# Weight tiles of 576 columns in place of 1152, and a new list of operations

## The chip, the core and the metric

The kernel runs on one core of a Trainium2 chip. The metric is the device time of one execution in microseconds. The engines are written as in the profile: PE is the matrix engine (TensorE), PEld its weight loads, DVE the vector engine, ACT the scalar engine, POOL the general engine (GpSimd), and SP the engine that issues the transfers.

## What is computed

Two halves of an output of 2048 rows and 1152 columns, all in float32. Columns 0 to 575 are a long convolution (an S4D state-space layer), columns 576 to 1151 a linear attention with a learned softmax feature map. The reference, cut to that:

```python
# left half: A_u is [1, 2048, 576]
P = jnp.exp((A * dt[:, None])[:, :, None] * pos[None, None, :])
K = 2.0 * jnp.einsum("dn,dnl->dl", C, P).real
y = jnp.fft.irfft(jnp.fft.rfft(u_t, L2) * jnp.fft.rfft(K, L2)[None], L2)[:, :, :L]
left = y + u * D_skip
# right half: x is [1, 2048, 576], 32 heads of 18
q, k, v = x @ wqkv                       # split in three
phi_q = softmax of q @ w_phi and of its negative, side by side (36 features)
phi_k = the same of k @ w_phi
kv = jnp.einsum("bhsf,bhsd->bhfd", phi_k, v);  z = phi_k summed over s
right = (phi_q @ kv / (phi_q @ z + 1e-6)) @ wo
```

## The kernel before, in words

The left half is done as a transform of 4096 points in stages of small matrix products. `u_first(k)` (16 of them, named u0 to u15 here) loads a block of the signal into a tile `ub`, multiplies it by `w1` on PE, copies the sums from PSUM to a tile `zi` and stores that in DRAM. `group(g)` (36, worked in 18 pairs, "group 0" to "group 17") makes a piece of the convolution's kernel: POOL adds phases, ACT takes sines and exponentials, DVE multiplies, and PE sums (`g0` are the products with `sel`, `g4` the sums). `k_first`, 16 `product` units and 16 `last` units finish the transform.

The right half is done in tiles of 128 rows. A **key tile** (16) loads a block of x transposed (`load_x`: tile `zo`, then split into a high part and a remainder in `x9`), multiplies it by the key weights and by the value weights (`gemm_halves`: two halves of 288 columns, 14 matrix products each: high weights with high x, low weights with high x, high weights with the low x), takes the double softmax, and adds into the 18x36 sums per head. Then `kv` writes those sums to DRAM and reads them back in another layout (`kvb`). A **query tile** (16) does the same with the query weights, divides, transposes, and multiplies by the output weights.

Weights come as a pair of tiles, high part and low part. `fold` makes the key (and later the query) weights: five blocks of `wkT` are loaded into staging tiles, PE multiplies each by the feature map (`fT`), ACT copies the high part out of PSUM and DVE subtracts to get the low part. `whole` makes the value (and later the output) weights: three thirds of 192 columns are loaded, ACT copies the high part and DVE or POOL subtracts. Before the change one pair `wh`, `wl` of 1152 columns holds keys in columns 0 to 575 and values in columns 576 to 1151. The pools keep one buffer for each of the two names, so the pair for queries and output takes the place of the pair for keys and values.

Nothing is scheduled at run time. Each operation gets a number as it is described, 2,506 in all, and the text `ORDER` lists these numbers in the order in which they are handed to the engines; an engine works its instructions strictly in that order. A number can carry `x` (run on the other engine of two allowed ones), `@` and digits (which of PSUM's eight banks its result takes) and `:n` (n filler products on PE ahead of it, 128x256 in bf16, on a tile of zeros, at L244; they write a bank that the operation then overwrites, or add zeros). The list before has 87 fillers: 20 and 11 of them at the start, between the blocks of the first fold, and 56 later.

Of the kernel before, what the change touches and what calls it, by code (L numbers as in the profile page):

```python
# [25 lines left out]
KEPT = 8  # L26
# [257 lines left out]
def body(tc, nc, i, out, ctx):  # L284
# [10 lines left out]
    tags({1: "zero ident w1 hp quarter dsk kvb fT cst wh wl ks sel pa ax ay mn ldc",  # L295
# [56 lines left out]
    def weights():  # L352

        return B("wh", [128, 5, 2 * D], F32R), B("wl", [128, 5, 2 * D], F32R)
# [27 lines left out]
    def whole(src, w, done, stage, eng):  # L382
        hi, lo = w

        def third(c):
            cs, half = slice(D + 192 * c, D + 192 * c + 192), Mark()
            wi = B(stage[c], [128, 5, 192])
            load_rows(wi, src, slice(192 * c, 192 * c + 192), 192)
            op("act", c_act(960), lambda: act.activation(hi.t[:, :, cs], wi.t, AF.Copy), r=[wi], w=[done[c], half], with_=[hi])
            op(eng, c_pool(960) if eng == "pool" else c_dve(960), lambda: (pool if eng == "pool" else dve).tensor_tensor(  # L390
                lo.t[:, :, cs], wi.t, hi.t[:, :, cs].bitcast(F32), op=ALU.subtract), r=[wi, half], w=[done[c]], with_=[hi, lo], lock=True)
# [39 lines left out]
    def gemm_halves(x, w, done, c0):  # L431
        ps = B("ps", [128, 2, 288], banks=2)
        for c, (cs, need) in enumerate(zip(halves, done)):
            gemm(x, w, need, ps, lambda c=c: ps.t[:, c], slice(c0 + cs.start, c0 + cs.stop))
# [33 lines left out]
    wkv, have_k, have_v = weights(), marks(5), marks(3)  # L468
    pl.at("fold", 0)
    fold(i["wkT"], wkv, have_k, ("e", "e", "cs", "e", "kvb"), [])  # L470
    pl.at("fold", 1)
    whole(i["wv"], wkv, have_v, ("zi", "zi", "cs"), "dve")
# [9 lines left out]
    def key_tile(t):  # L482
# [5 lines left out]
        pk = gemm_halves(x, wkv, (have_k[0:3], have_k[2:5]), 0)  # L488
        pc = gemm_halves(x, wkv, (have_v[0:2], have_v[1:3]), D)
# [47 lines left out]
    wqo, have_q, have_o = weights(), marks(5), marks(3)  # L537
    fold(i["wqT"], wqo, have_q, 5 * ("e",), [opened])
    pl.at("fold", 3)
    whole(i["wo"], wqo, have_o, 3 * ("e",), "pool")  # L540

    def query_tile(t):
        pl.at("query", t)
        ps = gemm_halves(load_again(t) if t < KEPT else load_x(t), wqo, (have_q[0:3], have_q[2:5]), 0)
# [49 lines left out]
        po = gemm_halves(o9, wqo, (have_o[0:2], have_o[1:3]), D)  # L594
# [399 lines left out]
0 1 2 4 3 1185 1125 5x 1124 34 35@0:20 69 1131 1135 1134 1132 36 39 37 44 1136 6 1133 1137 1138 1139 1140 38 1155 1141 40 1156 1147 359 27 8@2 1142  # L994
360 28@4:11 20 1168 51 13 47 1143 1144 1145 361x 1146 29 21@6 22 1106 362x 32 30 1148 1149 1154 1150 1151 1152 7 1105 33 31 15@0 52 25 23 9 24 279 41
26 14 45 18 10 1095 1108 1153 1157 16 17 1166 19 1158 364@4 48 11 1159 12 46 280 281x 49 1160 53 54 57@6 56 1192 42 1109 1167 1110 43 1161 1162 282
1107 1112 1163 60 61 1111 63 1113 62 363 368 299 1024 1164 1165 55 59@0 365@2 366 1035 367 72 1116 1114 1186 64 1118 369 1193 377 1115 300 58 1117
1119 370 371x 1120 1121 73 372 376 301x 1096@64 1194 1195 1098x 70 1187 1188 373 284@2 1196 65 1431 302 1197 1230 66 67 1189 1231 1190 1123 1097 1232
1223 283 1198 1224 1191 1036@40 303@6 288 1038x 177 1233 1037 287 374 68 1169 50@4 1200 304 1126 308 286@0 375x 1199 71 307 289 290 309 285 297x 378
1170 74x 1225 75x 1226 1201 1122 1179 1178 178 1227 1171 1182@52 1183@36 1211 1127 179x 1202 310 1128 1214 114 305@0 306 78@6 1203 1205 1204 1208 1206  # L1000
77 1435 296 180 291 379 1234 1039 76 1235 292 317 293 1228 182@0 311 1229 82 312 183 294 81 1207 313 295x 83 314 1184@52 1209@3 115 187 298 186 188
1213 1212 1215 116 1236 117 1237 181 339 1210x 189 195 1262 315x 184@6 316 119@0 120 1434 1432 1238 1129 1433 1172 1437 1217 1216 318 1218@5 1220@32
1173 1239 1174 1436 190x 185 1240 1438 84 1439 123 124 125 1268 126 1219 1243 1175 196 1241 90 127x 1269 85 1270 340 380 118 1244 191 341 342 79@0
1221@56 1271 1261 1263 1264 1272 1242 128 219 1249 80 1080 122@2 91 1246 1265 1266 343@0 1245 192 121 198 1273 193 1252 1222@57 220 1267 194 197 1275
86 129 87 88 1247@6 133 1248 221 1176 222 130 1251 1255 344 348 132 1274 224@2 223 131x 1254 1440 1250 1253 1276 227 89x 1177 228 199 200 229 1307 347
1277 346@6 134 1441 350 349 345 1259@52 351x 1258@30 319 230 201x 357 1256@1 92 356 231 1299 1306 1287 1290 1280 203@6 1279 93 1278 1281 1283 320 1257
1282 202 204 208 1308 1309 1442 232 352 207 209 1284 226@2 225 237 233 94 1081@06 1082 1083x 1084 1260@52 234 1310 1300 1130 1301 1285@3 210 1302 1303
1311 1304 1305 1312 1314x 95 96 1288 205@0 1286x 1289 235x 1338 1292 353 1293 1181 99@6 236 1313 1315 238 98 354 1180 239 1443 206 1291 1478 1296@53
355x 1316 1455 1317 103 102 104 1294@2 1295 211 321 212 217x 1100 1337 1339 1340 1101@60 358 1319 105 1345 1344 1346 1347 1297@25 1447 1102x 1103
1298@67 1320 100@0 106 1325 1328 1318 1321 1322 1348 1349 213 107 101 214 1323@5 322 323@2 1324x 108 1350 1070 1090 111 1341 240 324 241 112 1326 216  # L1010
1352 1327 1329 109 328 327 1342 97 1330 329 1331 259 1099 325@0 1343 1351 1454 326 215x 1071@26 242 260 1353 1456 110x 1332@5 218 1072 395 1444 1445
1446 1448 1449 1451 1450 135 1073 337 1452 1453 261x 1104 1091@26 1093x 1335@01 1092 1334@23 1457 1458 1459 1460 1354 330 331 244@6 1355 1333 1384
1357 262 136 1356 1358 1359 1360 1523 1461 1462 1463 1464 1465 243 1524 1525 1526 1387 246@2 1492 1094 247 1361@5 248 1362 113 156 1363 249 250 251x
332 245 257 157 1364@06 137x 1366 264@2 1336@56 333 334 158 1365x 263 265@0 1386 1389 1390 1531 336 1530 1385 252 267 268 269 1388 1050 1074 1479 335x
270 338 1369@62 1368 266 1367 1030 159 1493 1370x 277x 1532 1533 138 1527 1528 1529 1534 271 1535 1371 1379@26 1391@5 1381x 1380 1374@02 253 1537 272
273 1485 1536 1372 1373 276 256 1538x 1486 1375 274 1487 275x 1488 1376x 160 1383 141@6 140 1392 144 145 147 162@0 146 1489 1494 1495 1496 1497 1498
161 148 254 1490 1539 1382 1051@26 166 1053 165 278 1520@56 1052x 1540 167 1521@72 1378 440 1542 1541 168 255x 143@0 1500 1543 1544 1545 1546 149 1549
169 142 154 258 1552 1522@53 170 1031@60 1054 150 151 396 1040 1065 1032 1547@2 164@6 1551 1554 163 1033 174 1491 1499x 1548 1555 1377 153 171 172
1550 175x 1066@02 152x 398@6 397 1568 1553 1569 1501 1556@5 1068x 173x 399 1034 401 1067x 402 155 176 1482@23 475 1502 400 1503 417 1041@06 1570 1571
# [77 lines left out]
```

## Time and profile before

| | |
|---|---|
| time, median of 3 runs | 555.22 us (551.48 to 556.59) |
| the profiled execution's own time | 554.43 us |
| its span, first to last instruction | 552.5 us |
| mean granted PE clock | 0.990 |
| busy: PE, DVE, ACT, POOL | 534.8, 457.3, 377.2, 331.7 us |
| DMA, busy share of 16 engines | 64.8% |
| moved | 111.07 MB |

The profile is a record of one execution. Busy times of an engine are unions of its instructions. A matrix product's record is longer than its share of the engine, because products overlap in the array: the distance from one product's start to the next tells what it costs. "PEclk" is the clock that the throttle granted, as a share of the full clock. A row of the timeline has the start, the duration from the first start to the last end, engine, line, operation, tiles and count; in brackets stands the idle time ahead of it and what ended that.

### The profile page before, as it was taken

The page shows a single profiled execution, that of the slowest core. Times are in us where ns is not written, and L with a number is a line of the kernel's source. Part 1 is how long each engine was busy: PE and PEld are TensorE (multiplying, and loading weights), DVE is VectorE, ACT ScalarE, POOL GpSimd, SP SyncE. Part 2 cuts the span into 40 slices and gives each one's busy share as a digit, 9 for nine tenths or more (in the row PEclk, how much of TensorE's full clock was granted, in tenths as well). Part 3 has the DMA queues.
Part 4 walks back from the last instruction along what each step waited for, and adds up shares of the span by engine and source line. Part 5 has one row for each costly group of instructions (what it writes and reads, how often), then busy time and mean ns, then how long its engine had stood idle before and what let it go on. Part 6 is the DMA issues. An engine that isn't in the chain of part 4 may idle for free.

```text
span 552.5 us, 18491 instructions
## 1 busy us (share of the span) xinstructions
PE 534.8 (97%) x7777; PEld 439.9 (80%) x7777; DVE 457.3 (83%) x756; ACT 377.2 (68%) x546; POOL 331.7 (60%) x476
## 2 busy tenths in 40 slices
PE   6999999999999799999999999999999999999997
PEld 4999999989888677888887775777886866676986
DVE  6899999799978698999899988889885678676542
ACT  3789577998549789699699967968973343413332
POOL 2397767886499948782569778686534363444300
PEclk8999999999999998999999999999999999999999
DMA  8951710263464767726664678656788889998786
GB/s 216 296 173 53 259 59 26 94 194 135 147 171 151 234 214 245 216 86 193 210 205 142 212 231 243 200 173 224 210 249 245 232 268 303 283 310 259 264 255 160
DMA packets 90368, 111.07 MB, mean 201 GB/s; under 512 B 5938, under 2 KB 74546, under 8 KB 90286
## 3 DMA queue, kind: packets, MB, share of 16 engines
q1 hardware_dynamic: 90286, 109.90, 64.8%
q8 instruction: 61, 1.00, 0.7%
q14 instruction: 21, 0.17, 0.1%
HBM read 65.34 MB, written 44.54 MB: 199 GB/s over the span
## 4 chain that ended last, share of the span: by engine, by line
PE 83%; DVE 7%; ACT 4%; DMA 3%; issue 2%; SPq 1%; POOL 1%; DVEq 0%; POOLq 0%; ACTq 0%
PE psum L302 77%; PE psum L557 3%; DMA e<-in_wkT_dram 2%; PE psum L585 1%; PE psum L244 1%; ACT psum L819 1%; DVE cs L823 1%; DVE cs L824 1%; DMA fk<-in_fk_dram 1%; DVE ac L321 1%; ACT L819 1%; ACT fT L307 0%; DVE cs L826 0%; DVE cs L828 0%; DVE small L441 0%
## 5 line engine op out<-in xcount | busy, mean ns | idle before, releaser
L302 PE MATMUL psum<-wh,x 128*128 128x288 f32 x1152 | 247.7, 302 | 1.2 <-ACT cs L782 0.5
L302 PEld LDWEIGHTS psum<-wh,x 128*128 128x128 f32 x1152 | 188.5, 188 | 12.3 <-issue 6.2
L302 PE MATMUL psum<-wl,x 128*128 128x288 f32 x640 | 187.3, 295 | 0.0
L302 PEld LDWEIGHTS psum<-wl,x 128*128 128x128 f32 x640 | 120.5, 188 | 0.0
L765 POOL TENSOR_TENSOR cs<-cs,pi 128x128 int32<-128x128 int32 (+4 forms) x180 | 106.6, 601 | 7.3
L819 ACT ACTIVATE psum<-psum 128x512 f32<-128x512 f32 x108 | 59.2, 586 | 12.8 <-PE psum L302 12.3
L317 POOL TENSOR_TENSOR e<-e,small 128x1152 f32<-128x1152 f32 (+1 forms) x27 | 46.8, 1735 | 23.1 <-DVE small L321 9.9
L317 POOL TENSOR_TENSOR e<-small,e 128x576 f32<-128x576 f32 x27 | 31.8, 1177 | 33.3 <-DVE small L445 24.7
L823 DVE TENSOR_TENSOR cs<-psum,cs 128x1024 f32<-128x1024 f32 x36 | 43.6, 1215 | 9.0 <-ACT psum L819 8.9
L317 POOL TENSOR_TENSOR x<-zo,x 64x128 fp32r<-64x128 f32 (+1 forms) x36 | 31.4, 872 | 30.1 <-ACT x L401 26.8
L448 ACT ACTIVATE e<-e 128x1152 f32<-128x1152 f32 x32 | 37.2, 1166 | 14.5 <-POOL e L317 14.5
L317 POOL TENSOR_TENSOR ac<-ac 128x288 f32<-128x288 f32 x37 | 30.2, 828 | 24.4 <-DVE ac L321 21.2
L302 PEld LDWEIGHTS psum<-kvb,fT 126*128 126x128 f32 (+1 forms) x320 | 38.5, 189 | 7.5 <-issue 3.3
L824 DVE TENSOR_TENSOR cs<-psum,cs 128x1024 f32<-128x1024 f32 x36 | 43.7, 1213 | 0.2 <-PE psum L302 0.2
L302 PEld LDWEIGHTS psum<-cs 128*32 128x32 f32 x2304 | 34.1, 110 | 10.5 <-issue 6.0
L302 PE MATMUL psum<-kvb,fT 126*128 126x133 f32 (+1 forms) x320 | 42.0, 281 | 0.1
L302 PE MATMUL psum<-cs 128*32 128x64 f32 x2304 | 39.8, 221 | 0.9 <-DVE cs L824 0.8
L789 ACT ACTIVATE cs<-cs 128x1040 f32<-128x1040 int32 x36 | 38.3, 1063 | 0.2
L302 PE MATMUL psum<-kb,fk 128*64 128x288 f32 x256 | 35.9, 415 | 0.4 <-DMA fk<-in_fk_dram 0.4
L307 ACT ACTIVATE zi<-psum 128x576 f32<-128x576 f32 x35 | 22.0, 650 | 18.2 <-PE psum L302 11.2
L321 DVE TENSOR_TENSOR ac<-us,psum 128x1152 f32<-128x1152 f32 x24 | 31.7, 1348 | 1.7 <-PE psum L302 1.2
L307 ACT ACTIVATE ot<-psum 128x576 f32<-128x576 f32 x20 | 13.0, 650 | 27.0 <-PE psum L302 21.2
(151 smaller groups left out, 1033.4 us busy)
## 6 DMA issues: line engine op xcount, KB each, us to landing
dram<-zi SPq DMA_DIRECT2D x16, 576.0 KB
dram<-zi SPq DMA_DIRECT2D x32, 288.0 KB
kb<-dram SPq DMA_DIRECT2D x32, 288.0 KB
ub<-dram SPq DMA_DIRECT2D x32, 288.0 KB
dram<-zo SPq DMA_DIRECT2D x32, 288.0 KB
zo<-in_xT_dram SPq DMA_DIRECT2D x24, 320.0 KB
zi<-dram SPq DMA_DIRECT2D x12, 576.0 KB
ub<-in_u_dram SPq DMA_DIRECT2D x16, 288.0 KB
```

The lines of the kernel that those rows point to most:

```text
L244: self.matmul(t[0:cols, 0:n], self.zero.t[0:rows, 0:cols], self.data.t[0:rows].bitcast(BF16)[:, 0:n], start=not o[13], stop=not o[13], ski ...
L302: pe.matmul(o, l, r, start=start, stop=stop, skip_group_check=skip)
L307: op(("act", "dve"), (c_act(n), c_dve(n)), lambda e: act.activation(dst(), src(), AF.Copy) if e == "act" else dve.tensor_copy(dst(), src() ...
L317: op(eng, [c_dve(n[0]) if e == "dve" else c_pool(n[1]) for e in eng], lambda e: (dve if e == "dve" else pool).tensor_tensor(dst(), a(), b( ...
L321: op(eng, c_dve(n) if eng == "dve" else c_pool(n), lambda: e.tensor_tensor(dst(), a(), b(), op=alu), r=r, w=w, with_=with_, lock=eng == "p ...
L448: op("act", c_act(1152) + 40, lambda: act.activation(e.t, e.t, AF.Exp), r=[e], w=[e], table="exp")
L557: pe.transpose(tp.t[0:m, j - j0, :], e.t[:, sign, 7 * g:7 * g + GRP[g], :].rearrange("p h f -> p (h f)"), ident.t)
L765: op("pool", c_pool(2 * n * W), lambda n=n, j=j: pool.tensor_tensor(x()[:, :, :, n:2 * n], x()[:, :, :, 0:n], pi.t[:, j:j + 2, gs].bitcast ...
L789: act.activation(cs.t[:, 1], cs.t[:, 1].bitcast(I32), AF.Sin, scale=TURN)
L819: op("act", c_act(512), lambda b=b: act.activation(b.t, b.t, AF.Exp), r=[b], w=[b], table="exp")
L823: op("dve", c_dve(64 * W), lambda: dve.tensor_tensor(F(), both(M.t), F(), op=ALU.mult), r=[M, cs], w=[cs])
L824: op("dve", c_dve(64 * W), lambda: dve.tensor_tensor(E.t[:, :, :, 32:64], both(up.t), cs.t[:, :, :, 0:32], op=ALU.mult), r=[up, cs], w=[E])
```

## The change

`weights` now returns a pair of tiles of 576 columns under given names, and is called four times: keys take `wh` and `wl`, values `vh` and `vl`; later queries take `wh` and `wl`, output `vh` and `vl`. So each pair can be replaced when its own last reader is through, not when keys and values both are. The bytes held are the same.

```diff
-    tags({1: "zero ident w1 hp quarter dsk kvb fT cst wh wl ks sel pa ax ay mn ldc",
+    tags({1: "zero ident w1 hp quarter dsk kvb fT cst wh wl vh vl ks sel pa ax ay mn ldc",
...
-    def weights():
+    def weights(names):
-        return B("wh", [128, 5, 2 * D], F32R), B("wl", [128, 5, 2 * D], F32R)
+        return [B(n, [128, 5, D], F32R) for n in names]
...
-            cs, half = slice(D + 192 * c, D + 192 * c + 192), Mark()
+            cs, half = slice(192 * c, 192 * c + 192), Mark()
...
-    wkv, have_k, have_v = weights(), marks(5), marks(3)
+    wk, wv, have_k, have_v = weights(("wh", "wl")), weights(("vh", "vl")), marks(5), marks(3)
...
-        pk = gemm_halves(x, wkv, (have_k[0:3], have_k[2:5]), 0)
-        pc = gemm_halves(x, wkv, (have_v[0:2], have_v[1:3]), D)
+        pk = gemm_halves(x, wk, (have_k[0:3], have_k[2:5]))
+        pc = gemm_halves(x, wv, (have_v[0:2], have_v[1:3]))
...
-    wqo, have_q, have_o = weights(), marks(5), marks(3)
-    fold(i["wqT"], wqo, have_q, 5 * ("e",), [opened])
+    wq, wo, have_q, have_o = weights(("wh", "wl")), weights(("vh", "vl")), marks(5), marks(3)
+    fold(i["wqT"], wq, have_q, 5 * ("e",), [opened])
...
-0 1 2 4 3 1185 1125 5x 1124 34 35@0:20 69 1131 1135 1134 1132 36 39 37 44 1136 6 1133 1137 1138 1139 1140 38 1155 1141 40 1156 1147 359 27 8@2 1142
...
```

The 2,506 operations, what they compute and what they need are the same in both. `ORDER` is new throughout: the same numbers in another order, other banks, some operations on the other of their two engines (DVE has 757 operations for 756, ACT 455 for 453, POOL 469 for 472), and 122 fillers for 87: 26, 23 and 7 at the start, 66 later.

The first place is SP's queue at the start of the program. The rows are the first ten transfers: `cst` constants, `pa` parameters, `in_wkT` the five blocks of the key weights (into `kvb`, `e`, `cs`), `in_wv` the value weights' thirds, `in_xT` blocks of x, `w1` the transform's matrix. Before:

```order
L347 DMA cst_88<-in_sel_dram 128x214
L364 DMA kvb_100<-in_wkT_dram 72x640
L693 DMA pa_128<-in_par_dram 128x768
L350 DMA zi_139<-in_wv_dram 128x5x192
L364 DMA e_143<-in_wkT_dram 126x640
L350 DMA zo_158<-in_xT_dram 128x5x128
L364 DMA e_160<-in_wkT_dram 126x640
L364 DMA cs_181<-in_wkT_dram 126x640
L350 DMA zo_185<-in_xT_dram 128x5x128
L364 DMA e_187<-in_wkT_dram 126x640
```

And of the change:

```order
L347 DMA cst_90<-in_sel_dram 128x214
L693 DMA pa_92<-in_par_dram 128x768
L364 DMA kvb_107<-in_wkT_dram 72x640
L350 DMA zo_109<-in_xT_dram 128x5x128
L364 DMA cs_141<-in_wkT_dram 126x640
L364 DMA e_143<-in_wkT_dram 126x640
L364 DMA e_150<-in_wkT_dram 126x640
L350 DMA zo_153<-in_xT_dram 128x5x128
L607 DMA w1_155<-in_w1_dram 128x256
L364 DMA e_209<-in_wkT_dram 126x640
```

The last block of the key weights is the tenth transfer in both; ahead of it a third of the value weights (`zi`) is gone and `w1` has come.

The second place is the queue just behind, down to the last third of the value weights (`ub` is a block of the signal, `ac` and `ks` are parameters). Before, with the second third first and the last third at the end:

```order
L350 DMA cs_189<-in_wv_dram 128x5x192
L654 DMA ac_202<-in_mag_dram 128x640
L350 DMA zo_228<-in_xT_dram 128x5x128
L350 DMA zi_230<-in_wv_dram 128x5x192
L623 DMA ub_240<-in_u_dram 128x576
```

And of the change, where all three thirds stand:

```order
L350 DMA zi_243<-in_wv_dram 128x5x192
L623 DMA ub_247<-in_u_dram 128x576
L654 DMA ac_250<-in_mag_dram 128x640
L350 DMA zo_254<-in_xT_dram 128x5x128
L350 DMA zi_260<-in_wv_dram 128x5x192
L654 DMA ks_325<-in_mag_dram 128x640
L654 DMA ac_327<-in_mag_dram 128x640
L623 DMA ub_329<-in_u_dram 128x576
L350 DMA cs_378<-in_wv_dram 128x5x192
```

The last third was the 14th transfer and is now the 19th.

The third place is PE where the key tiles end: the last value product of the last key tile (key 5), `ub_` with `w1` is u8, and `fT_` with `e_` is the first block of the query weights' fold. Before:

```order
L302 MATMUL psum_73<-wh_136,x9_2303 128x288 x2
L302 MATMUL psum_73<-wl_150,x9_2303 128x288
L302 MATMUL psum_73<-ub_2762,w1_347 128x288 x4
L302 MATMUL psum_73<-fT_2104,e_2758 128x126 x5
L302 MATMUL psum_73<-cs_2813,cs_2369 32x64 x32
```

And of the change:

```order
L302 MATMUL psum_73<-vh_293,x9_2439 128x288 x2
L302 MATMUL psum_73<-vl_298,x9_2439 128x288
L302 MATMUL psum_73<-fT_2724,e_2726 128x126 x5
L302 MATMUL psum_73<-ub_2855,w1_155 128x288 x4
L302 MATMUL psum_73<-e_2720,v1_2774 19x36 x32
```

The fold's first block has moved ahead of u8; it stands behind the last value product in both.

182 lines of the change are left out of this document (92 added, 90 removed).

## Prediction

> **What bounds the kernel now.** I read the page first, then the busy times by stage, then the timeline where PE is not full.
>
> ```profile
> PE 534.8 (97%) x7777; PEld 439.9 (80%) x7777; DVE 457.3 (83%) x756; ACT 377.2 (68%) x546; POOL 331.7 (60%) x476
> ...
> PEclk8999999999999998999999999999999999999999
> ...
> PE 83%; DVE 7%; ACT 4%; DMA 3%; issue 2%; SPq 1%; POOL 1%; DVEq 0%; POOLq 0%; ACTq 0%
> ...
> L302 PE MATMUL psum<-wh,x 128*128 128x288 f32 x1152 | 247.7, 302 | 1.2 <-ACT cs L782 0.5
> ```
>
> PE is busy for 534.8 us, 97% of the span of 552.5, and 83% of the chain that ended last is PE. The change leaves every product with real data in place, so it can only win time in which PE idles, in which its clock is halved, or in which its products run further apart than they must. The group of weight products waited 1.2 us in 1152 products: once a tile of x is there, PE runs through. So I ask where PE idles. The columns are the length of the stage, then busy time and count of PE, PEld, DVE, ACT and POOL, the granted clock, the DMA share and GB/s.
>
> ```profile
> core 0: us, PE busy (x) PEld busy (x) DVE busy (x) ACT busy (x) POOL busy (x), PEclk, DMA share, GB/s
> 0.00:18.70 18.70, 14.08 (x82) 11.45 (x82) 11.67 (x34) 7.94 (x16) 4.82 (x12) 0.82 0.92 233
> 18.70:185.00 166.30, 165.01 (x2673) 150.16 (x2672) 152.75 (x228) 132.87 (x172) 124.43 (x179) 1.00 0.46 147
> 185.00:222.00 37.00, 31.88 (x571) 26.25 (x569) 30.14 (x59) 30.86 (x48) 26.12 (x40) 0.95 0.66 215
> 222.00:450.00 228.00, 225.49 (x3400) 175.52 (x3399) 201.19 (x337) 172.11 (x257) 145.68 (x215) 1.00 0.69 207
> 450.00:552.50 102.50, 98.38 (x1062) 76.54 (x1060) 61.56 (x104) 33.41 (x57) 30.61 (x33) 1.00 0.85 264
> ```
>
> PE idles 4.6 us before the first key product, 5.1 us while keys give way to queries (185 to 222), 4.1 us in the last stage, nearly all of it the last copy and store, and 1.3 and 2.5 us in the two long stretches. The clock is below full in the first and the third stage only. Those two are the places where a new list can win; they are also the places that the fillers mark. In the long stretches DVE is busy for 152.75 of 166.3 us and 201.19 of 228: it is the engine that would bind if PE did not.
>
> **The start.** The rows are PE's up to the first key product, and two transfers with their size.
>
> ```profile
> 1.46 4.24 PE L244 MATMUL psum<-ident,zero 128*128 128x256 bf16 x20 [1.46 <-DVE zero L340]
> 5.79 1.33 PE L302 MATMUL psum<-fT,kvb 72*128 72x72 f32 x10
> 9.95 0.79 PE L302 MATMUL psum<-fT,e 126*128 126x126 f32 x2 [2.83 <-DMA e<-in_wkT_dram]
> 10.54 2.55 PE L244 MATMUL psum<-ident,zero 128*128 128x256 bf16 x11
> 13.34 2.44 PE L302 MATMUL psum<-fT,e 126*128 126x126 f32 x10 [0.25 <-DMA e<-in_wkT_dram]
> 15.62 1.28 PE L302 MATMUL psum<-fT,cs 126*128 126x126 f32 x10
> 16.74 2.17 PE L302 MATMUL psum<-fT,e 126*128 126x126 f32 x18
> 18.67 0.38 PE L302 MATMUL psum<-wh,x 128*128 128x288 f32 x1
> ```
>
> ```profile
> zi<-in_wv_dram SPq DMA_DIRECT2D x2, 480.0 KB
> ...
> w<-in_w_dram SPq DMA_DIRECT2D x1, 128.0 KB
> ```
>
> PE waits for the key weights' blocks out of DRAM (2.83 and 0.25 us); 10 fold products take 2.44 us at half clock and 1.28 at full. In SP's order the last block is the tenth transfer before and after, but ahead of it a value third of 480 KB is gone and `w1` with 128 KB has come. That is 352 KB, or 360 kB, less; at the stage's 233 GB/s it is 1.5 us. The first key product then starts near 17.1 us in place of 18.67: **-1.5 us**. One end: 0, if ACT and DVE, which must still split each block, come last instead. Other end: -2.6, the 1.5 and another 1.1 because one block of 10 more runs at full clock (2.44 less 1.28). The 49 fillers ahead of the fold's later blocks keep PE without a pause, so the half-clock stretch that begins before 10 us should go; I count nothing for it, since the transfers come last. [...]
>
> The price of this move: the value weights come later. Their last third was the 14th transfer and is the 19th; `w1`, two `ub`, `ks` and one `ac` have passed it.
>
> ```profile
> ac<-in_mag_dram SPq DMA_DIRECT2D x2, 320.0 KB
> ub<-in_u_dram SPq DMA_DIRECT2D x2, 288.0 KB
> ...
> ks<-in_mag_dram SPq DMA_DIRECT2D x1, 320.0 KB
> ```
>
> ```profile
> 22.04 1.01 ACT L389 ACTIVATE wh<-zi 128x960 fp32r<-128x960 f32 x1 [0.39 <-DMA zi<-in_wv_dram]
> ```
>
> ```profile
> 25.00:50.00 25.00, 25.00 (x301) 23.03 (x299) 24.86 (x35) 21.16 (x25) 20.54 (x33) 1.00 0.41 130
> ```
>
> ```profile
> 517.34 1.86 PE psum L302 x14
> ```
>
> It lands at 22.04 now (ACT waited for it). 128+288+288+320+320 KB more are 1376 kB, 5.9 us at 233 GB/s: 27.9, and with ACT's 1.0 us and about as much on DVE it is ready near 30. PE's new list puts seven half products of keys and values and two `u` blocks between the first key product and the first that needs this third. The last row is from the chain in order of time: 14 products of one half take 1.86 us, 133 ns each. Seven halves are 13.0 us, two `u` blocks about 2 (the row of u0 below has 1.24, of which a part lies beside the next products): 17.1 + 15 = 32. It is hidden by 2 us, **0**; at the 130 GB/s of 25 to 50 us it would land at 32.6, be ready near 34.6 and cost 2.6.
>
> **Keys to queries.** `fold`'s first query block stands behind the last value product in both lists, so the split tiles free nothing earlier on PE.
>
> ```profile
> 184.97 1.19 PEld L302 LDWEIGHTS psum<-fT,e 126*128 126x128 f32 x10 [0.39 <-DVE v L307]
> ```
>
> ```profile
> 212.58 1.24 PE L302 MATMUL psum<-ub,w 64*128 64x288 f32 x8
> 213.44 0.62 PE L302 MATMUL psum<-sel,mg 64*128 64x512 f32 x2
> 214.83 0.50 PE L302 MATMUL psum<-sel,mg 64*128 64x512 f32 x2 [0.77 <-DVE zi L307]
> 215.50 1.58 PE L244 MATMUL psum<-ident,zero 64*128 64x256 bf16 x13 [0.17 <-DVE zi L307]
> 216.90 2.23 PE L302 MATMUL psum<-ub,w 64*128 64x288 f32 x8
> ```
>
> ```profile
> 213.89 0.36 SPq L623 DMA_DIRECT2D ub<-in_u_dram  x1
> ```
>
> Even before, that fold waited 0.39 us, and for a PSUM copy, not for a weight tile. The edit to the tiles is worth nothing by itself: **0**.
>
> What changes here is u4. Its block was issued at 213.89, and u4 began at 216.90 behind 13 fillers. PE had idled, the clock was halved just then, and u4 took 2.23 us where u0 took 1.24. The new list has 25 fillers there, at 1.58/13 = 0.12 us 3.0 us in all, right behind u0 and one pair of products. u4 so starts 0.5 + 3.0 = 3.5 us behind u0's end at 213.44, as before, but PE has not paused, and u4 runs at full clock: 1.24 for 2.23, **-1.0 us**. Bounds: -1.9 (the stage's clock of 0.95 is 0.05 x 37 us of clock lost) and 0, if the idle time only moves elsewhere in the stage. [...]
>
> **The rest.** 66 fillers in place of 56 after the start: 12 of the ten more are u4's, the others are two fewer, 0. One operation more or less on DVE, ACT and POOL is below 1 us on engines that PE does not wait for: 0. That the other 440 or so PE operations stand a few places earlier or later I cannot price from rows; PE idles only 1.3 and 2.5 us in the two long stretches, so little can be won, and a loss is bounded by the rival below.
>
> **The sum.** 552.5 - 1.5 - 1.0 = 550.0 us of span. The execution lay 1.9 us above its span (554.43), so 551.9; and the median of the runs shown, 555.22, lay 0.8 above that execution: **552.7 us**, 0.5% less than before.
>
> **The rivals.** *Both gains are made into new waits*, since the list was changed and not the work: the first key product still starts at 18.7 because ACT and DVE end last, the pause moves, 555 us. For it speaks that the tile split frees nothing; against it that a transfer of 480 KB really leaves the front of the queue.
>
> *More is won.* The start takes its other end (-2.6), the half clock goes fully (-1.9), and of the 5.1 us of idle time between 185 and 222 three go: -7.5, so 552.5 - 7.5 + 2.7 = 547.7, about 548 us. For it: the query weights' blocks are wholly re-ordered there. Against: it needs three gains at once.
>
> *DVE becomes the bound.* The place is the stretch of key tiles, 18.7 to 185, in which DVE is busy for 92% and idles 13.5 us.
>
> ```profile
> 150.00:175.00 25.00, 24.83 (x383) 21.52 (x384) 19.34 (x29) 16.61 (x22) 22.90 (x34) 1.00 0.60 167
> ```
>
> In this slice it idles 5.7 us and PE loses almost nothing, because DVE works ahead of PE's needs. If the new list puts pieces of a softmax earlier in DVE's queue than PE delivers their sums, DVE idles that much more and its lead is gone; one more slice like this, where PE needs what stands behind, is 5.7 us on PE, and the two gains are lost with it (the pauses that they remove come back as waits for DVE): 555.2 + 5.7 = 561 us, slower than before. It decides from the point where DVE idles more than its 13.5 us in the stretch by more than the 1.3 us that PE has there. For it: PE's wait for DVE costs nothing now only because of the list's order, and all of that is new. Against: the queue of PE has nearly the same units in the same sequence.
>
> **How the numbers follow.** I give the forecast 0.46, the new waits 0.14, the larger gain 0.22, the bound by DVE 0.18. One per cent, 5.6 us, is about what a measurement of this kernel can tell from no change: the three runs shown lie within 5.1 us. Below 549.7 lie the larger gain and a tail of the forecast, 0.27; above 560.8 most of the last rival, 0.17; between them 0.56. For 8 in 10 the range must reach both outer rivals' near side and the unknown ends (2.6 for the value third, 2.6 and 1.9 for the gains): 546 to 561 us.
>
> **What would show it.** Right: the first key product (`wh`, `x`) starts between 16.5 and 17.7 us; products of the fold run about 0.11 us apart from the second block on; no half clock near u4, and u4 takes 1.24 us; the value third's ACT copy ends before 30 us and PE does not wait for it; the stage of the key-to-query change has PE idle for 3.5 to 5 us, and the long stretches idle no more than 1.3 and 2.5. Wrong: the first key product at 18 us or later with DVE or ACT as what ended the wait; a stretch of fillers behind which the operation's inputs had long been there, which is filler time that PE pays for; or a fall of DVE's share in 18.7 to 185 with PE waiting for it. The prediction is also wrong if products run further apart than 133 ns in the long stretches, which no idle time shows.

## The result and the profile after

The changed kernel takes **551.14 us** (median of 20 runs, 546.96 to 553.84), the kernel before 554.83 us (20 runs, 551.33 to 557.59): ratio **0.9925, 95% interval 0.990 to 0.995**. A second series of the same program gave 0.9942 (0.9909 to 0.9974). The predicted 552.7 us lay between the two medians, and the change moved the time by less than 1%. In the series below, one execution each of the two kernels with a third moved (840.34 and 562.24 us) lay far above the other eleven and is left out of their medians and ratios.

The profiled execution of the changed kernel took 553.84 us, the longest of its 20, so the two spans hardly differ (552.5 and 552.1) although the medians are 3.7 us apart. The comparison of the traces is therefore one of places, and each place is looked up again in the traces of the experiments.

The lines of the page after that answer to those shown of before:

```profile
PE 534.9 (97%) x7812; PEld 442.8 (80%) x7812; DVE 458.7 (83%) x757; ACT 379.3 (69%) x547; POOL 325.0 (59%) x473
...
PEclk9999999999999999999999999999999999999999
...
PE 70%; DVE 11%; DMA 8%; ACT 6%; issue 3%; SPq 0%; POOL 0%; ACTq 0%; DVEq 0%
...
L302 PE MATMUL psum<-wh,x 128*128 128x288 f32 x576 | 126.0, 305 | 5.1 <-DVE x L317 3.2
```

PE has the same busy time, with 35 instructions more (the fillers). New are two things: PE is 70% of the chain that ended last in place of 83%, and the products with `wh`, which is now the keys' and queries' tile alone, wait 5.1 us in 576, where those of both halves had waited 1.2 us in 1152; DVE's part of a tile of x ended 3.2 of them.

The same stages as in the prediction (columns: length, then busy time and count of PE, PEld, DVE, ACT and POOL, granted clock, DMA share, GB/s):

```profile
0.00:18.70 18.70, 17.24 (x128) 15.09 (x129) 14.81 (x42) 9.41 (x19) 2.50 (x12) 1.00 0.92 252
18.70:185.00 166.30, 162.27 (x2637) 146.82 (x2636) 150.28 (x216) 129.39 (x167) 115.95 (x173) 0.99 0.46 143
185.00:222.00 37.00, 35.75 (x611) 30.39 (x610) 33.72 (x66) 35.66 (x55) 30.36 (x45) 1.00 0.73 240
222.00:450.00 228.00, 224.63 (x3443) 177.59 (x3441) 201.82 (x339) 171.87 (x252) 148.42 (x217) 1.00 0.69 208
450.00:552.10 102.10, 94.96 (x1002) 72.88 (x1000) 58.06 (x98) 32.96 (x57) 27.71 (x28) 1.00 0.84 257
```

PE idles 1.5, 4.0, 1.3, 3.4 and 7.1 us in the five stages, where it idled 4.6, 1.3, 5.1, 2.5 and 4.1 us. So 3.2 us went at the start and 3.9 us between keys and queries; 2.7, 0.9 and 3.0 us came in the other three. These are the five places to explain. (A filler counts as busy, so idle time alone does not say what a place costs.)

The start, PE's rows from the second block of the fold to the first key product:

```profile
10.41 1.28 PE L302 MATMUL psum<-fT,e 126*128 126x126 f32 x10
11.53 1.28 PE L302 MATMUL psum<-fT,cs 126*128 126x126 f32 x10
12.64 1.28 PE L302 MATMUL psum<-fT,e 126*128 126x126 f32 x10
...
14.66 1.38 PE L302 MATMUL psum<-fT,e 126*128 126x126 f32 x10
15.80 0.38 PE L302 MATMUL psum<-wh,x 128*128 128x288 f32 x1
```

These blocks run at 1.28 to 1.38 us for ten products, none at 2.44, and the first key product starts at 15.80 us in place of 18.67.

The new hole in the stretch of key tiles, in the timelines of PE, DVE and POOL:

```profile
68.23 0.85 PE L302 MATMUL psum<-wh,x 128*128 128x288 f32 x2 [3.17 <-DVE x L317]
```

```profile
62.90 2.23 DVE L321 TENSOR_TENSOR ax<-ax,ay 128x192 f32<-128x192 f32 x1
65.17 1.45 DVE L704 TENSOR_SCALAR ax<-ax 128x192 f32<-128x192 f32 x1
66.54 1.64 DVE L317 TENSOR_TENSOR x<-zo,x 128x512 fp32r<-128x512 f32 x1
```

```profile
62.60 2.32 POOL L317 TENSOR_TENSOR e<-e,small 128x1152 f32<-128x1152 f32 x1
...
65.29 1.21 POOL L515 MEMSET kvb<- 126x1330 f32 x1
```

PE has done the first two products of key tile 3 and waits for the part of x that DVE writes (x less its rounded value). DVE reaches it at 66.54 only: ahead of it in its queue stand operations on phases (`ax`), 192 elements wide, and two of these take 2.23 and 1.45 us. ACT had written the rounded value at 56.4 us, so its input was there ten microseconds before. The products behind the wait then run at half clock: the pair above takes 0.85 us, where a pair takes 0.43 us from 71.5 us on, and the granted clock of 60 to 80 us is 0.91. That is so in five of the six traces with this wait (0.83 to 0.91; 1.00 in that of the new list with two tiles).

### The profile page after: what moved, and what is told of

Same layout as the page of the kernel before. It is cut to its first block, busy times and chain, and to the rows that moved or that the text cites. A ratio compares the mean times of both kernels' runs of the same rounds, so it can differ in the third digit from the quotient of the medians.

```text
span 552.1 us, 18539 instructions
## 1 busy us (share of the span) xinstructions
PE 534.9 (97%) x7812; PEld 442.8 (80%) x7812; DVE 458.7 (83%) x757; ACT 379.3 (69%) x547; POOL 325.0 (59%) x473
## 4 chain that ended last, share of the span: by engine, by line
PE 70%; DVE 11%; DMA 8%; ACT 6%; issue 3%; SPq 0%; POOL 0%; ACTq 0%; DVEq 0%
PE psum L302 64%; PE psum L557 3%; DMA ff<-in_ff_dram 2%; DMA x<-xd 1%; PE psum L244 1%; PE psum L585 1%; DMA dram<-zo 1%; DMA out_dram<-ot 1%; DMA zo<-in_xT_dram 1%; DVE small L450 1%; DMA dram<-zi 1%; DMA pa<-in_par_dram 1%; DVE x L317 1%; DVE small L441 1%; DVE e L317 1%
## 5 line engine op out<-in xcount | busy, mean ns | idle before, releaser
L302 PE MATMUL psum<-wh,x 128*128 128x288 f32 x576 | 126.0, 305 | 5.1 <-DVE x L317 3.2
L302 PE MATMUL psum<-vh,x 128*128 128x288 f32 x576 | 123.6, 301 | 0.9 <-DVE zo L307 0.8
L302 PEld LDWEIGHTS psum<-wh,x 128*128 128x128 f32 x576 | 95.2, 190 | 12.5 <-issue 4.6
L302 PEld LDWEIGHTS psum<-vh,x 128*128 128x128 f32 x576 | 94.2, 188 | 7.0 <-issue 3.1
L302 PE MATMUL psum<-wl,x 128*128 128x288 f32 x320 | 94.4, 297 | 0.0
L302 PE MATMUL psum<-vl,x 128*128 128x288 f32 x320 | 93.7, 295 | 0.0
L317 POOL TENSOR_TENSOR e<-e,small 128x576 f32<-128x576 f32 (+1 forms) x28 | 46.9, 1675 | 32.0 <-DVE small L321 21.9
L302 PEld LDWEIGHTS psum<-wl,x 128*128 128x128 f32 x320 | 60.8, 190 | 0.0
L302 PEld LDWEIGHTS psum<-vl,x 128*128 128x128 f32 x320 | 60.2, 188 | 0.0
L453 POOL TENSOR_TENSOR o<-e 128x576 f32<-128x576 f32 x16 | 21.1, 1319 | 38.6 <-ACT e L448 37.8
```

The source lines that it names most:

```text
L302: pe.matmul(o, l, r, start=start, stop=stop, skip_group_check=skip)
L317: op(eng, [c_dve(n[0]) if e == "dve" else c_pool(n[1]) for e in eng], lambda e: (dve if e == "dve" else pool).tensor_tensor(dst(), a(), b( ...
L453: op("pool", c_pool(470), lambda: pool.tensor_tensor(pair.t, e.t[:, :, :, 0:9], e.t[:, :, :, 9:18], op=ALU.add), r=[e], w=[pair], lock=True)
```

## Experiments

All ratios are to the kernel before, which ran on the same chip in the same series. Intervals are 95%.

| kernel | median, us (runs) | ratio | interval |
|---|---|---|---|
| changed kernel, again | 552.05 (12) | 0.9942 | 0.9909 to 0.9974 |
| new list, two tiles | 552.38 (12) | 0.9933 | 0.9904 to 0.9962 |
| old list, four tiles | 555.22 (12) | 1.0005 | 0.9979 to 1.0031 |
| changed, old start fillers | 552.85 (12) | 0.9952 | 0.9921 to 0.9982 |
| new list, then old | 558.60 (12) | 1.0057 | 1.0026 to 1.0087 |
| old list, then new | 552.92 (12) | 0.9972 | 0.9947 to 0.9996 |
| key 3 mended | 548.87 (6) | 0.9883 | 0.9847 to 0.9919 |
| changed, no late fillers | 551.74 (8) | 0.9943 | 0.9919 to 0.9968 |
| before, a third moved | 554.18 (11) | 0.9971 | 0.9946 to 0.9996 |
| before, third and ACT moved | 556.60 (11) | 1.0000 | 0.9973 to 1.0027 |
| before, one product moved | 552.47 (12) | 0.9951 | 0.9926 to 0.9975 |
| key 3 mended further | 547.89 (6) | 0.9856 | 0.9823 to 0.9889 |

**The changed kernel again.** No edit.

> The changed kernel once more, unaltered, for a second trace of it: its first trace holds a wait of PE for DVE at 64.6 us that the trace of before does not hold. Theory 1 (an accident of timing): DVE there ran three short operations beside POOL, one of 128x192 in 2.23 us where its like takes 0.35, and the wait goes or shrinks below 1 us in another execution; the execution is then some 3 to 5 us shorter, 545 to 549 us of span. Theory 2 (the list itself puts the operations of the phases ahead of the second part of x): the wait is there again with 3 to 5 us. Either way the first key product (psum<-wh,x) starts at 15.8 us, give or take 0.3, and u4 takes 1.24 us.

```profile
69.76 0.53 PE L302 MATMUL psum<-wh,x 128*128 128x288 f32 x2 [3.15 <-DVE x L317]
```

The wait is there again, 3.15 us: theory 2, the list makes it. Four of the other kernels below keep the new list unaltered at this place, and all four show it, with 3.15 to 3.17 us. The expectation on the start missed: the first key product came at 17.35 us, so the start varies by 1.5 us from one execution to the next.

**List and tiles apart.** The first kernel has the code of before with the new list, the second the code of after with the old list.

```diff
 wkv = weights()        # two tiles, both halves in each
-ORDER = (old list)
+ORDER = (new list)
```

> The new list with the old two weight tiles of 1152 columns. Theory 1 (the list does all of it): ratio to before 0.992, as the whole change, first key product at 15.8 us, PE idle for 1 to 2 us between 185 and 222. Theory 2 (the tiles free the query weights earlier): ratio 1.000, and PE idles for about 5 us between 185 and 222 as before, since the fold of the query weights then waits for the value half of the old tile.

```diff
 wk, wv = weights(("wh", "wl")), weights(("vh", "vl"))
-ORDER = (new list)
+ORDER = (old list)
```

> The old list with the four tiles of 576 columns. Theory 1 (the list does all of it): ratio to before 1.000 within 0.002, the wait of PE in front of the query fold as before. Theory 2 (the tiles free the query weights earlier): ratio 0.993 to 0.996, with 2 to 4 us less idle time of PE between 185 and 222.

The list with the old tiles gives 0.9933, first key product at 16.30 us; the tiles with the old list give 1.0005, with the old waits. Theory 1: **the list does all of it, and the tiles do nothing by themselves.**

**Fillers of the start.**

```diff
-35@0:26 ... 28@2:23 ... 14@0:7
+35@0:20 ... 28@2:11 ... 14@0
```

> The changed kernel with the fillers of the start as in the kernel before: 20, 11 and none in place of 26, 23 and 7. Theory 1 (the gain at the start is the order of the transfers; the fillers only stand where PE would wait): the first key product starts at 15.5 to 16.1 us, time within 0.3 us of the changed kernel. Theory 2 (the fillers hold the clock): the clock falls to half in the first 16 us again, one to three of the blocks of ten fold products take 2.44 us in place of 1.28, and the first key product starts 1.2 to 2.9 us later, at 17 to 18.7 us. Theory 3 (part of the fillers is paid for): it starts up to 2 us earlier, 13.8 to 15.4 us.

```profile
10.66 1.38 PE L302 MATMUL psum<-fT,e 126*128 126x126 f32 x10 [2.05 <-DMA e<-in_wkT_dram]
11.88 2.08 PE L302 MATMUL psum<-fT,cs 126*128 126x126 f32 x10
13.75 3.27 PE L302 MATMUL psum<-fT,e 126*128 126x126 f32 x20
16.77 0.38 PE L302 MATMUL psum<-wh,x 128*128 128x288 f32 x1
```

With fewer fillers PE waits 2.05 us for the block, and part of the next thirty products runs at half clock: 6.11 us from that block to the first key product (10.66 to 16.77), against 5.39 in the changed kernel (10.41 to 15.80) and 5.35 to 5.97 in the six other traces with all fillers of the new start. So the half clock of theory 2 is back in part, and the fillers are worth 0.1 to 0.8 us in this stretch; but the first key product comes at 16.77 us, within the range of the seven with all fillers (15.80 to 17.35), and the time cannot be told from theirs. Most of the gain is not the fillers': this start is still earlier than those of the old list (17.22 to 18.83 us).

**Halves of the two lists.** The operations up to the eleventh key tile (about 180 us) come in the order of one list, those that are left in the order of the other.

```diff
 ORDER = first 740 words of the new list
-        + the rest of the new list
+        + what is left, in the order of the old list
```

> Four tiles; the new list up to the eleventh key tile (about 180 us), from there the operations that are left in the order of the old list. What the parts of the traces so far add up to: the start is 2 to 3 us shorter than before, the wait of PE for x at 65 us costs 3.4 to 4.8 us, and the two waits of PE at 188 and 193 us (3.4 us) are those of before. Theory 1 (the parts add): 0 to 2 us slower than before, ratio 1.000 to 1.004, although it has the whole of the gain at the start. Theory 2 (the gain of the change is the start, as the prediction has it, and the rest moves nothing): ratio 0.994 to 0.996.

```profile
PE psum L302 <- ACT zi L307: 2.2, 2, 1.9
```

The mirror image takes the first 742 words of the old list.

> Four tiles; the old list up to the eleventh key tile (about 180 us), from there the operations that are left in the order of the new list, with its 25 fillers in front of u4. Theory 1 (the parts add): first key product at 18 to 18.7 us, no wait for x at 65 us, the two waits at 188 and 193 us gone or under 1 us together, so 3 to 4.5 us faster than before, ratio 0.992 to 0.995. Theory 2 (the gain is the start): ratio 0.998 to 1.001, since only the u4 term of 1.0 us is left.

```profile
PE psum L302 <- POOL e L317: 3.8, 1, 3.8
```

New then old is slower than before, 1.0057, a little more than the 1.004 of theory 1, although its first key product comes at 16.68 us: the gain at the start is smaller than the loss at key tile 3, and the wait for ACT between keys and queries (above, in the view of waits of 160 to 222 us: us in total, times, longest) is back. **Taken together, the gain of the whole change comes from behind 180 us.** Old then new gives 0.9972, less than expected. Its joint costs time: at 169 us PE waits 3.8 us for POOL, which is in neither list alone, and the granted clock behind it is 0.86 from 160 to 185 us, so this ratio alone says little about the sum; its waits between 185 and 222 us are 1.4 us, in the changed kernel 1.2.

**Key tile 3 mended.** One operation, DVE's part of x of key tile 3, stands before the phases in place of behind them.

```diff
-... 83 298 181 1436 1209@2 ... 1437 1438 1439 1261 116x 117 1215 ...
+... 83 298 181 116x 1436 1209@2 ... 1437 1438 1439 1261 117 1215 ...
```

> The changed kernel with one operation of the list moved: DVE's part of the tile x of key tile 3 (x<-zo,x 128x512) stands ahead of the four operations on phases (128x192) and the softmax operations behind which it stood, in place of behind them. Theory 1 (PE waits at 65 us because of that place in DVE's queue): the wait falls from 3.4 to 4.8 us to below 0.7 us, and the time is 3 to 4.5 us below the changed kernel's, ratio to before 0.985 to 0.988. Theory 2 (DVE is late there as a whole, from its collisions with POOL, and the lost time only moves): PE waits as long somewhere between 60 and 80 us, ratio 0.992 to 0.994.

```profile
71.98 0.40 PE L302 MATMUL psum<-vh,x 128*128 128x288 f32 x1 [2.16 <-DVE e L321]
```

```profile
64.48 2.24 DVE L321 TENSOR_TENSOR ax<-ax,ay 128x192 f32<-128x192 f32 x1
```

Between the theories: 0.9883. The wait for x is gone, but 2.16 us stand 4 us further on, now for a softmax operation, since DVE still spends 2.24 us (and then 1.45) on the short operations. In the second mending these stand behind the next sums and maxima:

```diff
+116x ahead of 1436, as above
-... 1436 1209@2 ... 1437 1438 1439 ... 186 187 ... 188 ...
+... 1436 1209@2 ... 186 187 ... 188 1437 1438 1439 ...
```

> The mended list with three more operations of DVE moved: the phases' operations of 128x192 (pa, ax, ax) that took 0.34, 2.24 and 1.45 us beside POOL's product of e (2.26 us) and its fill of kvb (1.20 us) stand behind the next four operations on sums and maxima. Theory 1 (DVE lost those 3 us to what POOL did at the same time): both short operations of ax take under 0.6 us at their new place if POOL does something else there, PE's wait for DVE at 72 us falls from 2.2 us to below 0.5, and the time is 1.5 to 2.5 us below the mended kernel's, ratio to before 0.983 to 0.986. Theory 2 (they take long wherever they stand, or the next long operation of DVE beside POOL is slow in their place): the wait stays above 1.5 us, ratio 0.987 to 0.990.

```profile
64.47 1.22 DVE L824 TENSOR_TENSOR cs<-psum,cs 128x1024 f32<-128x1024 f32 x1 [0.35 <-ACT psum L819]
...
69.21 0.36 DVE L321 TENSOR_TENSOR ax<-ax,ay 128x192 f32<-128x192 f32 x1
69.60 0.26 DVE L704 TENSOR_SCALAR ax<-ax 128x192 f32<-128x192 f32 x1
```

```profile
64.17 2.19 POOL L317 TENSOR_TENSOR e<-e,small 128x1152 f32<-128x1152 f32 x1 [0.33 <-ACT cs L782]
...
67.79 1.18 POOL L317 TENSOR_TENSOR e<-small,e 128x576 f32<-128x576 f32 x1
70.86 1.29 POOL L317 TENSOR_TENSOR x<-zo,x 128x512 fp32r<-128x512 f32 x1 [1.90 <-ACT x L401]
```

Theory 1. Where POOL does nothing (68.97 to 70.86), the same two operations take 0.36 and 0.26 us; PE waits nowhere between 60 and 74 us, and the kernel stands at **0.9856, the fastest of all**, 7.5 us below the one before. By the two ratios (0.9925 and 0.9856) the place had cost about 0.7% (by their intervals about 0.3 to 1.1%), as much as the change gained with it. The traces agree: from the first key product to the first block of the query weights' fold it is 169.2 to 170.5 us in the five traces that have the new list throughout, fillers apart, 167.5 us after the first mending and 165.7 us after the second.

**Late fillers.**

```diff
-1483@45:5  1076@46:2  1046@60:25  1420@7:7  638@2:15  2119@24:5  1822@45:6  2268@24:1
+1483@45    1076@46    1046@60     1420@7    638@2     2119@24    1822@45    2268@24
```

> The changed kernel without the 66 fillers behind the start (those of the start, 26, 23 and 7, stay). Theory 1 (as the prediction has it, they stand where PE would wait and hold its clock): PE waits at their places for as long as the fillers took, 2.6 us ahead of u4 and 1.6 us at 306 us, the clock is halved behind u4, u4 takes up to 2.23 us in place of 1.24, and the time is the changed kernel's or up to 2 us above it. Theory 2 (the inputs of what follows were there before, and PE pays for the fillers): PE goes straight on at those places, the clock stays full, and the time is 2 to 5 us below the changed kernel's.

```profile
216.90 2.29 PE L302 MATMUL psum<-ub,w 64*128 64x288 f32 x8 [3.23 <-ACT psum L819]
```

Theory 1 in its lower half: PE waits 3.23 us where 25 fillers stood and u4 takes 2.29 us, but 0.9943 cannot be told from the changed kernel. At these places, as at 307 us, where PE now waits 1.32 us, the fillers are not paid for; what they save is below what these series resolve, although the granted clock fell to a mean of 0.992 over its eight executions, from 0.998 over the changed kernel's 20.

**The start by itself, in the old list.** First only the transfer, then ACT's copies with it.

```diff
-... 36 39 37 44 1136 6 ... 20 1168 51 13 47 1143 ...
+... 36 39 37 1136 6 ... 20 1168 51 13 44 47 1143 ...
```

> The kernel before, with one transfer of its list moved: the first third of the value weights (480 KB) stands behind the last block of the key weights in SP's order, in place of ahead of the first; fillers and everything else as before. Theory 1 (the start's gain is that transfer): 480 KB at 233 GB/s are 2.1 us less ahead of the last block; the first key product, at 17.2 to 18.7 us in the three traces with the old front of the list, starts at 15.6 to 16.8 us, and the ratio is 0.995 to 0.998. Theory 2 (it needs the other moves of the front or the fillers too): at 17.2 us or later, ratio 0.998 to 1.002.

```profile
13.88 1.35 PE L302 MATMUL psum<-fT,e 126*128 126x126 f32 x10 [0.55 <-DMA e<-in_wkT_dram]
16.02 0.37 PE L302 MATMUL psum<-wh,x 128*128 128x288 f32 x1 [0.79 <-ACT wh L389]
```

```diff
+44 moved as above
-... 26 14 45 18 10 ... 16 17 ... 364@4 48 11 1159 ...
+... 26 14 18 10 ... 16 17 ... 364@4 11 45 48 1159 ...
```

> The kernel before with the first third of the value weights moved in SP's order as in the run before, and with ACT's copies of the first two thirds (wh<-zi and wh<-cs, 1.0 us each) moved behind ACT's last copy of the key weights' fold. In the run before, the last block came early enough, but ACT stood in front of the moved third (0.67 us) and copied it (1.00 us) ahead of the fold's own copies, and PE lost 2.5 us behind its first key product. Theory 1 (the start's gain needs the transfer and ACT's order together): the first key product starts at 15.0 to 16.5 us and PE waits less than 0.5 us behind it, ratio to before 0.994 to 0.997. Theory 2 (DVE's order of the fold's second copies holds it as well): a wait of 0.7 us or more for DVE stays behind the first key product, ratio 0.997 to 1.000.

```profile
12.62 1.35 PE L302 MATMUL psum<-fT,e 126*128 126x126 f32 x10 [0.23 <-DVE ax L321]
15.90 0.37 PE L302 MATMUL psum<-wh,x 128*128 128x288 f32 x1 [1.93 <-DVE wl L374]
...
17.39 0.68 PE L302 MATMUL psum<-wh,x 128*128 128x288 f32 x2
```

The last block now comes at 13.88 and 12.62 us, and the first key product at 16.02 and 15.90. But ACT in the first kernel, and DVE in the second, are late with the block's copies, and the products behind are 0.24 us apart (0.48 for two), at half clock. The 29th weight product starts at 22.34 and 22.06 us; in the four traces with the old front it starts at 21.04 to 22.65, mean 22.04. What the transfer wins is gone after 28 products; with the whole new front these 28 end at 19.71 to 21.25 us, mean 20.55 in seven traces, so there the lead of 1.5 us is kept. By its numbers the first kernel meets its theory 1 (16.02 us, ratio 0.9971), which had not looked behind the first key product; the second meets theory 2 (PE waits 0.72 us for DVE behind that product, ratio 1.0000). The two intervals overlap, and the first alone allows a gain of 0.5%. That an early block is useful only with ACT's and DVE's order behind it and PE kept busy is what the rows suggest; no kernel here has the transfer with those orders and nothing else.

**One product between keys and queries, in the old list.** The product of group 7 moves behind the sums of the last two key tiles.

```diff
-... 1553 1569 1501 1556@5 1068x ... 155 176 1482@23 475 ...
+... 1553 1569 1501 1068x ... 155 176 1482@23 1556@5 475 ...
```

> The kernel before, with one operation of its list moved: the product of group 7 (psum<-cs, 64 products, 1.10 us), which PE runs ahead of the last two key tiles' sums at 186 us, stands behind them and behind the first pair of products of group 6 (psum<-sel,mg), as in the new list. Theory 1 (that product is what covers ACT's copy of u3 out of PSUM in the new list): the wait of PE for ACT zi at 193 us falls from 1.85 us to 0.4 to 1.0 us. Theory 2 (the wait is ACT's own lateness, its table load of 1.28 us and its order): it stays at 1.5 us or more. The time moves by at most 0.3%, so the trace decides.

PE's timeline of the kernel before at this place, then with the product moved:

```profile
187.20 0.86 PE L302 MATMUL psum<-e,v 128*19 128x36 f32 x77
189.58 0.64 PE L302 MATMUL psum<-e,v 128*19 128x36 f32 x51 [1.52 <-issue]
...
193.70 2.50 PE L302 MATMUL psum<-fT,e 126*128 126x126 f32 x20 [1.85 <-ACT zi L307]
```

```profile
188.06 0.41 PE L302 MATMUL psum<-cs 128*32 128x64 f32 x11
189.26 0.98 PE L302 MATMUL psum<-cs 128*32 128x64 f32 x53 [0.79 <-issue]
...
192.16 2.50 PE L302 MATMUL psum<-fT,e 126*128 126x126 f32 x20 [0.52 <-ACT zi L307]
```

Theory 1: the wait for ACT falls from 1.85 to 0.52 us. ACT's work for group 6 (a table load of 1.28 us and two operations, 1.07 us together) begins when its first products are done; with group 7's 64 products between those and `u3`, ACT gets through it while PE works. The time fell to 0.9951, more than the 0.3% allowed for. The two waits are not the whole account: from u8 to the first product of the first query tile, the same work takes 18.55 us here and 21.12 us in the kernel before (20.81 to 22.67 in four traces with the old list), and of this the shorter stop without an event (0.79 us) need not be owed to the move. By the medians of the ratios one moved word of the old list brings two thirds of what the whole new list brings; by the intervals it is between a quarter and all.

## Why the prediction was right, and where it was not

The time was near (552.7 forecast, 551.14 measured) and inside the range. That was in part luck. The steps were right in part; the sum was saved by two terms that it lacked and that nearly cancel: a gain between keys and queries and a loss at key tile 3.

*The tiles, 0.* Right, and shown: 1.0005 for the tiles without the list, 0.9933 for the list without the tiles.

*The start, -1.5 us.* Right in size. In four traces with the old front of the list the first key product starts at 17.22 to 18.83 us, mean 18.22; in seven with the whole new front at 15.80 to 17.35, mean 16.64: 1.6 us. (The mean lies in the 16.5 to 17.7 us that the prediction named, the 15.80 us of the profiled execution does not.) The step's reason was incomplete. It counted 352 KB less ahead of the last block and took ACT and DVE not to come last; moving 480 KB alone brought, behind the first key product, the end that the prediction gave as 0, "if ACT and DVE, which must still split each block, come last instead". The new list had moved those copies too, which the prediction did not work out. Of the 49 fillers that it puts ahead of the fold's later blocks, 26 stand ahead of the first block; 23 and 7 stand ahead of later ones.

*The value weights' last third, 0.* Right.

```profile
28.40 1.15 DVE L390 TENSOR_TENSOR vl<-cs,vh 128x960 fp32r<-128x960 f32 x1
```

It was ready on DVE at 29.6 us (on ACT at 27.0), as forecast near 30, and PE did not wait for it.

*u4, -1.0 us.* Wrong as a term. u4 did run at full clock, but it did so with 13 fillers too. With the 13 of the old list, four tiles:

```profile
211.43 1.24 PE L302 MATMUL psum<-ub,w 64*128 64x288 f32 x8
...
215.76 1.13 PE L302 MATMUL psum<-ub,w 64*128 64x288 f32 x7
```

and with the 25 of the changed kernel:

```profile
211.48 1.13 PE L302 MATMUL psum<-ub,w 64*128 64x288 f32 x8
...
216.47 1.13 PE L302 MATMUL psum<-ub,w 64*128 64x288 f32 x7
```

From u0's begin to u4's end these are 5.5 and 6.1 us; in the trace that the prediction read it was 6.6 (212.58 to 219.13). u4 was at half clock in two of six traces with 13 fillers, in one of one without any, and in none of seven with 25. That PE keeps its clock where it has not paused, as the term took it, no run shows by itself: behind nearly the same waits (0.77 and 0.17 us in the kernel before, 0.78 and 0.16 us in that with the four tiles) u4 was at half clock in the first and at full clock in the second. The term was read from one execution, and such a half clock comes and goes with the execution. That 25 fillers keep it away is possible (none in seven against two in six), but no gain at this place is shown.

*Idle time between 185 and 222 us, 3.5 to 5.* This is the step that failed most: it was 1.3 us, and 1.2 to 2.6 us in the seven traces with the new list and its fillers here. The prediction asked there only for u4 and for the tile edit. It had seen that `fold` waited, and that the query weights' blocks were re-ordered, and put this into a rival. Two waits of before, 1.85 us for ACT and 1.52 us that no event ends, are gone from this place in the changed kernel:

```profile
PE psum L302 <- DVE e L321: 0.8, 1, 0.8
PE psum L302 <- DVE e L307: 0.4, 1, 0.4
```

These are all of PE's waits of 185 to 222 us after. The same work can be compared by its own ends, whatever the fillers: the fold, u8, two more `ub` blocks, the sums and 192 `cs` products, up to the first product of the first query tile. Before:

```profile
183.80 1.24 PE L302 MATMUL psum<-ub,w 64*128 64x288 f32 x8
...
204.92 0.40 PE L302 MATMUL psum<-wh,x 128*128 128x288 f32 x1
```

After:

```profile
185.81 1.28 PE L302 MATMUL psum<-fT,e 126*128 126x126 f32 x10
...
202.88 0.38 PE L302 MATMUL psum<-wh,x 128*128 128x288 f32 x1
```

That is 21.12 and 17.07 us; 19.89 to 22.67 us in five traces with the old order here, mean 21.2, and 17.06 to 18.49 us in eight with the new, mean 17.6: 3.6 us, where the prediction had 1.0. The moved product removed most of the first wait in the old list as well.

*The long stretches, no more than 1.3 and 2.5 us idle.* Wrong: 4.0 and 3.4. In the second a stop of 1.28 us that no event ends, just before 416 us, is more than the difference. In the first, what came is the mechanism of the third rival, "DVE becomes the bound", at one place: phases earlier in DVE's queue than PE can bear, DVE's share of 18.7 to 185 fallen from 152.75 to 150.28 us, and PE waiting for it, the sign that the prediction named. It had priced this at 5.7 us and let both gains be lost with it; it costs 3.2 us of waiting and more behind it (two mendings together win 0.7%), and the gains stayed. Part of what is behind it is the half clock, at most 1.8 us by an estimate from the granted clock of 0.91 over 60 to 80 us (0.09 of 20 us); the prediction's last sign, products further apart than 133 ns in a long stretch, is there too, 0.24 us between products at 69 us.

*"More is won."* Its part between 185 and 222 us was there and larger than its three microseconds; without the loss at key tile 3 the changed kernel reaches 547.89, the 548 of this rival. So both outer rivals happened at once, and the forecast lies between them. By places, in means over the traces, the first key product comes 1.6 us earlier; from there to the fold (in the old list to u8 just ahead of it) the new list takes 4.9 us more (169.8 us in five traces, 165.0 in three with the old list and start), most of it the place at key tile 3; up to the first query product it takes 3.6 us less; and from there to the last weight product 2.2 us less (342.5 us in eight traces, 344.7 in six). That is 2.5 of the 3.7 us. The last of these terms was not taken apart and swings from 338.9 to 345.3 us with the new list, so the first trace, with 345.3, shows nothing of it. The 3.0 us more of idle time in the last stage of that trace are waits for the transfer of `ff` (2.1 us), DVE (0.8) and ACT (0.4), where before it was 0.4 us for a transfer; the second mending, with the same list there, idles 5.9 us.

## To carry to other kernels

When a list that sets the order is rewritten, the terms read off from the diff (a transfer, a filler count) can be the small ones, as here: look at each wait of the old trace for whether something now stands inside it, and at each operation of an engine that works ahead for what now stands in front of it. An operation whose inputs were ready 10 us before it runs, and whose output PE waits for, can be moved in one line; moving it, and then three short operations behind it, brought as much again as the whole change. A stall or a half clock in one execution is not a term before a second execution shows it too.

## What the runs showed of the hardware

**Short DVE operations beside POOL.** `ax<-ax,ay` (128x192, both inputs and the output in SBUF) took 2.23 and 2.24 us beside POOL's product of e (2.32 and 2.26 us) and 0.36 us where POOL was idle; the single-input operation behind it 1.45 us beside POOL's fill of `kvb` (1.21) and 0.26 alone; `x<-zo,x` 1.64 us beside POOL's `e<-small,e` (1.17) and 0.68 alone. In the kernel before, `ax<-ax,ay` started at 229.90 us, 0.15 us ahead of a product of e on POOL (1.21), and took 0.34 us. `cs<-psum,cs`, with one input in PSUM, was not slowed: it took 1.22 us inside POOL's product of e of 2.19 us (64.17 to 66.36 us, in the rows of the second mending), and 1.21 elsewhere. What makes the short operations slow beside POOL, no run took apart.

**A stop that belongs to a count.** The 1.52 us "issue" wait at 189.58 us stands at the same number of PE's matmuls, 2902, in the six traces named here, whichever products stand there. Busy time and count from the start to 188.40 us, inside the stop, in the kernel before and with the product moved:

```profile
0.00:188.40 188.40, 182.16 (x2902) 164.42 (x2902) 167.42 (x264) 143.13 (x190) 132.25 (x198) 0.98 0.51 157
```

```profile
0.00:188.40 188.40, 183.31 (x2902) 165.59 (x2902) 167.42 (x265) 143.16 (x191) 131.73 (x194) 0.98 0.51 157
```

Both have 2902 matmuls ahead of it; before it falls among the `e,v` products, afterwards among the `cs` products. Four other traces with the old list up to here (the four tiles alone, the two with the third moved, and old then new) have the same count. The stop takes 1.44 to 2.38 us where `e,v` products stand there (four traces) and 0.79 and 0.20 us where `cs` products do. In the changed kernel no stop is seen at that count, but a stop of 1.28 us that no event ends stands just before 416.12 us, among short `ks,w` products (0.39 us in its second trace). What the stop is, no run took apart.
